# Rounds of two slots in an attention stage: which PSUM banks the units take by turns, and where scores and conversions stand

## The chip, the cores and the metric

One core of a Trainium2 chip runs the whole program. Its engines are TensorE (PE, with its weight loads shown apart as PEld), VectorE (DVE), ScalarE (ACT), GpSimd (POOL) and SyncE (SP), which issues the DMAs. The metric is the device time of one execution in microseconds (us); the time of a kernel is the median of its runs.

## The reference

Attention with heads mixed before and after the softmax, then two MLPs on the result (B=4, H=12, S=448, D=64; 1792 tokens of 768, hidden 2048; everything in float32):

```python
scores = scale * np.matmul(q, k.transpose(0, 1, 3, 2))
scores = np.einsum('bhij,hg->bgij', scores, w_pre)
scores = scores - np.max(scores, axis=-1, keepdims=True)
attn = np.exp(scores)
attn = attn / (np.sum(attn, axis=-1, keepdims=True) + 1e-09)
attn = np.einsum('bhij,hg->bgij', attn, w_post)
x = np.matmul(attn, v)                      # then (tokens, heads * D)
x = np.maximum(x @ w1_in, 0) ** 2 @ w1_out
h = x @ w2_in
out = (h * np.clip(h + 3, 0, 6) / 6) @ w2_out
```

## The kernel before, in words

**Stages.** The four batches are worked in two groups of two (`gi` 0 and 1). Each group has an attention stage (about 4 to 220 us and 690 to 890 us of the span) and then its MLPs (`Mlps` to 690, `Blocks` to the end, which saves products by sums of blocks). In the MLPs each matrix is split into a high and a low part, and three products stand for one in float32.

**Chunks, tiles, slots.** A group's queries come in eight chunks of 110 or 118 rows. A chunk is cut into tiles of 10 query rows times 12 heads (a last one of 8 rows), 90 tiles in all; a slot is two tiles, 45 slots. A tile goes through these steps:

- *Score* (`score`, line 186; products in line 183): for a chunk and two heads, eight matmuls into two PSUM banks; ACT copies one bank (line 189) and DVE the other (line 191) into the chunk's buffer `s`. Six scores make a chunk. There are two buffers `s`, so chunk 3 writes where chunk 1 was, and its copies must wait until SP's DMAs have fetched chunk 1's last tiles.
- *Fetch* (`fetch`, line 210): a DMA on SP reads a tile's rows of all heads out of `s` into `t`, five slots ahead.
- *Premix* (`premix`, line 222): eight matmuls for a slot with `w1f`, into two banks; then DVE's maximum (`top`, line 237), ACT's exponential with its sum (`soft`, line 246), DVE's reciprocal (`invert`, 254 and 255), POOL's weights scaled by it (`scale`, line 266).
- *Postmix* (`postmix`, line 278): eight matmuls for a tile, into one bank; `keep` copies it into `a`, for even tiles on ACT (line 293), for odd ones on DVE (line 295).
- *Values* (`values`, line 308): once a chunk's tiles are kept, 48 matmuls with V into each of two banks, which DVE copies into `xr` (line 318). The last chunk's come after the rounds, as `closing`.

**Banks.** PSUM has eight banks, held as four tags of two: "bm" and "by" take the premixes by turns, "bs" the scores, "bo" the postmixes, and, in rounds, the values too. A unit that takes a tag waits until the copies of what was there before have read it.

**Order.** Everything is written in the order in which each engine does it; nothing is rescheduled. From slot 1 (first group) or 3 (second group) on, `two_slots` (line 454) works two slots as one round: 22 rounds in the first group and 21 in the second. A round has two premixes, up to three scores, the values if a chunk is complete, and then a quad: the four postmixes of its two slots. Below, M is a premix of a slot, S a score, V a chunk's values, O one tile's postmix. A round with two scores is M S M S O O O O on PE; in one with three, the third comes after the O. `plan` (line 363) spreads a chunk's scores evenly over the slots from five before the end of the chunk two back to six before its own first tile, and puts the DMAs of q three slots ahead of their score. In a round, the first score of its first slot comes after the first premix, the next after the second, and any others at the round's end.

**Weights.** The first group's MLP weights come as 64-bit floats and are converted to 32 bits (`convert`, lines 658 to 667) and split into `wh` (ACT, line 693) and `wl` (DVE, line 694). For the first unit this is done in three steps during the attention stage (`early`, line 631), one in each round with values from slot 23 on: loads (chunk 3's values), first half (chunk 4's), second half, store and split (chunk 5's). In those rounds the step stands behind the values, and ahead of `soft(m + 3)`, the exponentials of the round's second premix.

**The entry into the MLP.** After `run` come the closing values, then the hidden products (`hidden`, line 730; matmuls in line 736): 18 matmuls for a block of 128 hidden units and one batch.

Of the kernel before, what the change touches and what calls it, by code (L numbers as in the profile page):

```python
# [70 lines left out]
def attention_mlp_kernel(ctx: ExitStack, tc, qT, kT, v, w_pre, w_post, mask, w1_in, w1_out, w2_in, w2_out, outT):  # L71
# [63 lines left out]
    class Attention:  # L135
        def __init__(self, gi):
            self.gi = gi
            self.batches = list(range(gi * NB, gi * NB + NB))
            self.chunks = [(b, ci) for b in self.batches for ci in range(len(CH))]
            self.tiles, self.first, self.tb = [], [], []  # L140
            for c, (b, ci) in enumerate(self.chunks):
                r0, n, nt, nl = CH[ci]
                self.first.append(len(self.tiles))
                self.tiles += [(c, t, RI if t < nt else nl) for t in range(nt + (nl > 0))]
            self.first.append(len(self.tiles))
            self.n = -(-len(self.tiles) // 2)
            self.live, self.ss, self.aa, self.ap, self.xr = {}, {}, {}, None, None
            self.ks, self.n_raw, self.raw, self.at, self.late = None, 0, None, {}, False
            if gi == 0:
                self.first_opening()  # L150
            self.plan()
# [34 lines left out]
        def score(self, c, k):  # L186
            out = [bank("bs" if self.ap else "bm", f"ps_s{self.gi}_{c}_{2 * k + e}") for e in range(2)]
            self.products(c, k, out)
            nc.scalar.activation(self.s(c)[:, 2 * k, :], out[0][:, :S], AF.Copy)  # L189
            if self.ap:  # L190
                nc.vector.tensor_copy(self.s(c)[:, 2 * k + 1, :], out[1][:, :S])
            else:
                nc.scalar.activation(self.s(c)[:, 2 * k + 1, :], out[1][:, :S], AF.Copy)
# [77 lines left out]
        def postmix(self, i):  # L271
            if i >= len(self.tiles):
                return
            c, t, ni = self.tiles[i]
            pt, w2s = self.live.pop(("w", i))
            o = bank("bo", f"ps_o{self.gi}_{i}")
            for q in range(JC):
                nc.tensor.matmul(  # L278
                    o[:JP, q * G * ni:(q + 1) * G * ni], lhsT=pt[:, q * JP:(q + 1) * JP],
                    rhs=w2s[:, :G * ni], start=True, stop=True)  # L280
            self.live["o", i] = o
# [81 lines left out]
        def plan(self):  # L363
# [11 lines left out]
            for c in range(1, nch):  # L375
# [5 lines left out]
                if c == 1:  # L381
                    when = [2 * k // nk for k in range(nk)]
                else:
                    low = last[c - 2] - FETCH + 1
                    when = [low + k * (top - low + 1) // nk for k in range(nk)]
                for j in range(2):
                    put(when[j * KP] - 3, self.fetch_q, c, j)
# [11 lines left out]
            for v in range(NV):  # L399
                put(1 + 3 * v, self.fetch_v, self.batches[0], v)  # L400

# [52 lines left out]
        def two_slots(self, m, early):  # L454
# [11 lines left out]
            visits = [[w for w in work if w[0].__name__ == "score"] for work in (first, second)]  # L466
            for (fn, (c, k)) in visits[0][1:]:
                assert self.first[c] // 2 - FETCH > m
            ready = [visits[0].pop(0)] if visits[0] else []
            rest = visits[0] + visits[1]  # L470

            def visit(work):
                if work:
                    fn, args = work.pop(0)
                    fn(*args)
# [11 lines left out]
            visit(ready)  # L487
# [12 lines left out]
            visit(rest)  # L500
            on(self.top_of, m + 3, 1)
            for fn, args in first + second:
                if fn.__name__ == "values":
                    fn(*args, "bo")
                    if early:
                        early.pop(0)()
                    on(self.soft, m + 3)
            self.postmix(2 * m)
# [3 lines left out]
            self.postmix(2 * m + 1)  # L512
            self.keep(2 * m + 1)
            on(self.scale, m + 2, 1)
            if ("m", m + 3) in self.live:
                self.soft(m + 3)
            self.postmix(2 * m + 2)
# [3 lines left out]
            self.postmix(2 * m + 3)  # L521
            self.keep(2 * m + 3)
            on(self.scale, m + 3, 1)
            while rest:
                visit(rest)
            do("fetch_v", first + second)

        def run(self, ap, behind, beside=None, early=None):
# [6 lines left out]
            for m in range(self.n + 1):  # L535
                two = m >= PAIRED[self.gi > 0] and (m - PAIRED[self.gi > 0]) % 2 == 0 and m + 1 < self.n
# [62 lines left out]
    class Mlps:  # L599
        def __init__(self, gi, att):  # L600
# [6 lines left out]
            self.arena, self.ready, self.late, self.scaled, self.unit0 = None, {}, [], set(), None  # L607
# [21 lines left out]
        def early(self):  # L629
# [16 lines left out]
            return [load, lambda: convert(0), lambda: (convert(1), self.store(0), self.split(0))]  # L646
# [83 lines left out]
        def hidden(self, which, fc, e, wh, wl, hp=None):  # L730
            cols = slice(e * S, (e + 1) * S)
            hp = hp or bank("bm", f"ps_h{self.gi}_{which}_{fc}_{e}")
            k = 0
            for c in range(KC):
                for lw, rw in ((wh, self.xh), (wl, self.xh), (wh, self.xl)):
                    nc.tensor.matmul(  # L736
                        hp[:, :S], lhsT=lw[:, c * P:(c + 1) * P], rhs=rw[:, c, cols],
                        start=(k == 0), stop=(k == 3 * KC - 1))
                    k += 1
            return hp  # L740

# [53 lines left out]
        def run(self, mp, behind):  # L795

            rest = None
            for n, (kind, which, m, _) in enumerate(self.units):
# [19 lines left out]
                if kind == "h":  # L818
# [14 lines left out]
                    hp = self.hidden(which, m, 0, wh, wl)  # L833
# [32 lines left out]
    class Blocks(Mlps):  # L866
# [117 lines left out]
        def early(self):  # L984
            return []

# [261 lines left out]
    with tc.manual_schedule():  # L1248
# [5 lines left out]
        for gi in range(groups):  # L1254
            last = gi > 0 and gi == groups - 1
            mlp = (Blocks if last else Mlps)(gi, att)
            with tc.tile_pool(name=f"ap{gi}", bufs=1, reuse_waits="tile") as ap:
                rest = att.run(ap, mlp.opening(), mlp.beside if last else None, mlp.early())

                for m, step in enumerate(att.closing()):  # L1260
# [90 lines left out]
```

## Time and profile before

| | |
|---|---|
| median of three runs | 1301.23 us (1299.87 to 1302.35) |
| the profiled execution, its own time | 1300.42 us |
| its span | 1298.6 us |
| granted clock of PE, mean | 0.999 |
| busy: PE, PE's loads | 1278.5 us (98%), 1097.8 us (85%) |
| busy: DVE, ACT, POOL | 918.9 (71%), 653.5 (50%), 270.5 us (21%) |
| chain that ended last, by engine | PE 95%, DMA 2%, ACT 1%, DVE 1% |
| the same chain, attention's lines | O 12%, S 6%, V 6%, M 5% |

The span is what the hardware profiler recorded between the first and the last instruction of one execution; the execution's own time is 1.8 us longer. Busy time of an engine is that in which at least one of its records is open. PE's matmuls overlap, so a matmul that waits a little for its bank leaves no gap in the busy time; a row of a timeline joins equal instructions that follow each other, and "x32" says how many. The time from the start of one such row to the start of the next shows what the busy time doesn't. In brackets stands the idle time of the engine before a row, and what ended it.

### The profile page before, as it was taken

What the parts mean: (1) busy time and instruction counts of PE and PEld (TensorE: products, weight loads), DVE (VectorE), ACT (ScalarE), POOL (GpSimd) and SP (SyncE); (2) the same over time, 40 slices, a digit from 0 to 9 for tenths busy, and PEclk for the clock granted to TensorE, in tenths of its full rate; (3) what the DMA queues carried; (4) which work ended last, traced back from release to release, by engine and by line L of the source; (5) the groups of instructions that cost most, each with busy time, mean ns of one, the idle gap of its engine ahead of it and who ended that gap; (6) DMA issues with size and microseconds to landing.
All of it is one profiled execution on the core that took longest, in us unless ns stands there. A gap on an engine that the chain in (4) does not pass through costs nothing.

```text
span 1298.6 us, 23568 instructions
## 1 busy us (share of the span) xinstructions
PE 1278.5 (98%) x8788; PEld 1097.8 (85%) x8788; DVE 918.9 (71%) x1554; ACT 653.5 (50%) x1260; POOL 270.5 (21%) x349
## 2 busy tenths in 40 slices
PE   8999989999999999999999999999999999999998
PEld 4677668999999999998895677778999999999998
DVE  5666666777766587875555666664977897799975
ACT  5555555555322355542425554555768555446652
POOL 2111113343200033310101334352001120001422
PEclk9999999999999999999999999999999999999999
DMA  6644422767786676677774776666877856785442
GB/s 201 185 135 149 131 105 99 206 202 208 240 279 186 191 227 202 206 233 234 257 250 152 230 230 219 195 213 231 275 246 222 272 184 203 232 286 175 126 132 95
DMA packets 131090, 261.10 MB, mean 201 GB/s; under 512 B 13728, under 2 KB 99872, under 8 KB 130976
## 3 DMA queue, kind: packets, MB, share of 16 engines
q1 hardware_dynamic: 127520, 254.09, 61.3%
q10 hardware_dynamic: 3456, 5.51, 1.2%
q8 instruction: 69, 1.13, 0.4%
q14 instruction: 45, 0.37, 0.1%
HBM read 151.02 MB, written 69.99 MB: 170 GB/s over the span
## 4 chain that ended last, share of the span: by engine, by line
PE 95%; DMA 2%; ACT 1%; DVE 1%; issue 0%; SPq 0%; ACTq 0%; POOL 0%; DVEq 0%
PE ps_h L736 18%; PE ps_a L750 18%; PE ps_w L1046 16%; PE ps_y L1146 16%; PE ps_o L278 12%; PE ps_s L183 6%; PE ps_v L308 6%; PE ps_m L222 5%; DMA t<-s 1%; DMA q<-in_dram 1%; ACT p L246 0%; DMA first<-in_dram 0%; DVE mx L237 0%; ACT a L293 0%; ACT s L189 0%
## 5 line engine op out<-in xcount | busy, mean ns | idle before, releaser
L278 PEld LDWEIGHTS ps_o<-w2s,p 128*112 128x112 f32 x1440 | 157.4, 178 | 40.2 <-issue 30.0
L278 PE MATMUL ps_o<-w2s,p 128*112 128x120 f32 (+1 forms) x1440 | 172.9, 274 | 7.8 <-ACT a L293 6.8
L750 PE MATMUL ps_a<-gh,wh 128*128 128x448 f32 x384 | 140.2, 365 | 0.0
L750 PE MATMUL ps_a<-gh,wl 128*128 128x448 f32 x384 | 138.7, 361 | 0.0
L694 DVE TENSOR_TENSOR wl<-arena,wh 128x768 fp32r<-128x768 f32 x63 | 61.8, 981 | 105.4 <-ACT wh L693 102.1
L266 POOL TENSOR_SCALAR w2s<-w2f,rz 128x120 f32<-128x120 f32 x180 | 65.3, 370 | 333.0 <-DVE rz L255 212.0
L1135 POOL TENSOR_TENSOR o<-gi,o 128x448 fp32r<-128x448 f32 x28 | 57.4, 2052 | 336.8 <-ACT o L1130 230.0
L246 ACT ACTIVATE p<-ps_m,mx 128x448 f32<-128x448 f32 x180 | 112.6, 632 | 24.9 <-DVE mx L237 21.8
L237 DVE TENSOR_REDUCE mx<-ps_m 128x1 f32<-128x448 f32 x180 | 105.2, 616 | 16.8 <-PE ps_m L222 16.1
L693 ACT ACTIVATE wh<-arena 128x768 fp32r<-128x768 f32 x63 | 52.8, 839 | 121.1 <-PE ps_a L750 113.7
L1146 PE MATMUL ps_y<-o,wx 128*128 128x448 f32 x504 | 105.4, 362 | 0.0
L1146 PEld LDWEIGHTS ps_y<-o,wx 128*128 128x128 f32 x504 | 94.5, 187 | 6.3
L189 ACT ACTIVATE s<-ps_s 128x448 f32<-128x448 f32 x87 | 47.1, 541 | 103.2 <-PE ps_s L183 98.1
L1146 PE MATMUL ps_y<-o,wh 128*128 128x448 f32 x336 | 98.7, 362 | 0.0
L728 POOL TENSOR_TENSOR gl<-g,gh 128x448 fp32r<-128x448 f32 x40 | 53.6, 1341 | 205.3 <-ACT gh L727 159.7
L295 DVE COPY a<-ps_o 112x480 f32<-112x480 f32 (+1 forms) x90 | 58.9, 654 | 47.5 <-PE ps_o L278 47.2
L293 ACT ACTIVATE a<-ps_o 112x480 f32<-112x480 f32 (+1 forms) x90 | 51.7, 575 | 75.6 <-PE ps_o L278 75.5
L222 PE MATMUL ps_m<-t,w1f 64*64 64x448 f32 x720 | 87.5, 546 | 1.8 <-POOL w2s L266 1.3
L183 PE MATMUL ps_s<-k,q 64*64 64x448 f32 x672 | 86.3, 555 | 2.6 <-ACT s L189 2.6
L750 PE MATMUL ps_a<-gl,wh 128*128 128x448 f32 x240 | 86.7, 361 | 0.0
L308 PEld LDWEIGHTS ps_v<-a,v 112*64 112x64 f32 x1536 | 73.8, 137 | 11.6 <-issue 9.2
L750 PEld LDWEIGHTS ps_a<-gh,wh 128*128 128x128 f32 x384 | 72.1, 188 | 10.0 <-issue 5.6
(117 smaller groups left out, 2892.0 us busy)
## 6 DMA issues: line engine op xcount, KB each, us to landing
arena<-in_dram SPq DMA_DIRECT2D x63, 768.0 KB
t<-s SPq DMA_DIRECT2D x176, 210.0 KB
keep<-arena SPq DMA_DIRECT2D x63, 384.0 KB
pr<-keep SPq DMA_DIRECT2D x88, 192.0 KB
wr<-sums_in SPq DMA_DIRECT2D x64, 192.0 KB
wr<-sums_out SPq DMA_DIRECT2D x64, 192.0 KB
low<-wl SPq DMA_DIRECT2D x28, 384.0 KB
wr<-keep SPq DMA_DIRECT2D x48, 192.0 KB
```

What stands on the lines that cost most here:

```text
L183: nc.tensor.matmul(out[e][to:to + half_p, :S], lhsT=q[own, to:to + half_p], rhs=keys[own], start=True, stop=True)
L222: nc.tensor.matmul(out[a][to:to + half_p, :S], lhsT=w1f[own], rhs=t[own], start=True, stop=True)
L237: nc.vector.reduce_max(mx[:, a:a + 1], out[a][:, :S], axis=AX.X, negate=True)
L246: nc.scalar.activation(pt, o[:, :S], AF.Exp, bias=mx[:, a:a + 1], accum_out=z[:, a:a + 1])
L266: nc.gpsimd.tensor_scalar(w2s[:, :G * ni].rearrange("p (g i) -> p g i", g=G), w2f[:, a, :, :ni], rz[:, a:a + 1], 1.0, op0=ALU.mult, op1=AL ...
L278: nc.tensor.matmul(o[:JP, q * G * ni:(q + 1) * G * ni], lhsT=pt[:, q * JP:(q + 1) * JP], rhs=w2s[:, :G * ni], start=True, stop=True)
L308: nc.tensor.matmul(xo[e * D:(e + 1) * D, k * n:(k + 1) * n], lhsT=self.v[:, q, g, :], rhs=self.aa[c][:, q, g, :n], start=(q == 0), stop=(q ...
L694: nc.vector.tensor_tensor(out=wl, in0=self.wr(n), in1=f(wh), op=ALU.subtract)
L736: nc.tensor.matmul(hp[:, :S], lhsT=lw[:, c * P:(c + 1) * P], rhs=rw[:, c, cols], start=(k == 0), stop=(k == 3 * KC - 1))
L750: nc.tensor.matmul(acc[d, e][:, :S], lhsT=lw[:, wc], rhs=rw[fc, e], start=(fc == 0 and k == 0), stop=(fc == NF - 1 and k == 2))
L1046: nc.tensor.matmul(to[:, :S], lhsT=lw[:, wc], rhs=rw, start=(d == 0 and j == 0), stop=(d == DB - 1 and j == 2))
L1146: nc.tensor.matmul(self.acc[d][:, :S], lhsT=lw[:, wc], rhs=rw, start=(u == 0 and q == 0 and j == 0), stop=(u == NU // 2 - 1 and q == UF - ...
```

## The change

In rounds, scores, values and both pairs of a quad's postmixes take "bs" and "bo" by turns, by one counter (`in_turn`); before, scores always had "bs", and values and postmixes "bo". The two products of a pair share a tag, as before.

The places of a chunk's scores come from a list (`places`): each slot's possible places in a round, after the first premix (V), after the second (W) or at the end (C), and the last six before the chunk's first fetch are used; the first of them that lies in the slot of the earlier chunk's last fetches is left out. The q DMAs are issued four slots ahead, not three.

In rounds with values, the order is now: exponentials of the second premix, conversion step, values (before: values, conversion step, exponentials). The early conversion has four steps, as `split(0)` is one of its own, so they fall to the values of chunks 3, 4, 5 and 6.

`begin` puts the first nine of the first block's 18 hidden matmuls ahead of the closing values, in the first group alone.

```diff
+        def in_turn(self):
+            self.turn = 1 - self.turn
+            return ("bs", "bo")[self.turn]
+
-        def score(self, c, k):
-            out = [bank("bs" if self.ap else "bm", f"ps_s{self.gi}_{c}_{2 * k + e}") for e in range(2)]
+        def score(self, c, k, tag=None):
+            out = [bank(tag or ("bs" if self.ap else "bm"), f"ps_s{self.gi}_{c}_{2 * k + e}") for e in range(2)]
...
-        def postmix(self, i):
+        def postmix(self, i, tag="bo"):
...
-            o = bank("bo", f"ps_o{self.gi}_{i}")
+            o = bank(tag, f"ps_o{self.gi}_{i}")
...
-                    low = last[c - 2] - FETCH + 1
-                    when = [low + k * (top - low + 1) // nk for k in range(nk)]
+                    places = self.places(last[c - 2] - FETCH + 1, top)[-nk:]
+                    when = [slot for slot, _ in places]
+                    self.place.update({(c, k): place for k, (_, place) in enumerate(places)})
                 for j in range(2):
-                    put(when[j * KP] - 3, self.fetch_q, c, j)
+                    put(when[j * KP] - 4, self.fetch_q, c, j)
...
+        def rounds(self, m):
+            m -= PAIRED[self.gi > 0]
+            return None if m < 0 else m % 2
+
+        def places(self, low, top):
+
+            out = []
+            for m in range(low, top + 1):
+                at = self.rounds(m)
+                if at is None:
+                    out += [(m, "A")] * (2 if m == low + 1 else m > low)
+                    continue
+                if at == 0 or m > low:
+                    out.append((m, "VW"[at]))
+                if at == 1:
+                    out.append((m, "C"))
+            return out
...
-            visits = [[w for w in work if w[0].__name__ == "score"] for work in (first, second)]
-            for (fn, (c, k)) in visits[0][1:]:
-                assert self.first[c] // 2 - FETCH > m
-            ready = [visits[0].pop(0)] if visits[0] else []
-            rest = visits[0] + visits[1]
-
-            def visit(work):
-                if work:
-                    fn, args = work.pop(0)
-                    fn(*args)
+            visits = [w for w in first + second if w[0].__name__ == "score"]
+
+            def visit(place):
+                for fn, args in visits:
+                    if self.place[args] == place:
+                        fn(*args, self.in_turn())
...
             on(self.premix, m + 2)
             on(self.top, m + 2, False)
-            visit(ready)
+            visit("V")
...
-            visit(rest)
+            visit("W")
             on(self.top_of, m + 3, 1)
             for fn, args in first + second:
                 if fn.__name__ == "values":
-                    fn(*args, "bo")
+                    on(self.soft, m + 3)
                     if early:
                         early.pop(0)()
-                    on(self.soft, m + 3)
-            self.postmix(2 * m)
+                    fn(*args, self.in_turn())
+            tag = self.in_turn()
+            self.postmix(2 * m, tag)
...
-            self.postmix(2 * m + 1)
+            self.postmix(2 * m + 1, tag)
...
+            tag = self.in_turn()
             if ("m", m + 3) in self.live:
                 self.soft(m + 3)
-            self.postmix(2 * m + 2)
+            self.postmix(2 * m + 2, tag)
...
-            self.postmix(2 * m + 3)
+            self.postmix(2 * m + 3, tag)
...
-            while rest:
-                visit(rest)
+            visit("C")
...
-            return [load, lambda: convert(0), lambda: (convert(1), self.store(0), self.split(0))]
+            return [load, lambda: convert(0), lambda: (convert(1), self.store(0)), lambda: self.split(0)]
...
-        def hidden(self, which, fc, e, wh, wl, hp=None):
+        def hidden(self, which, fc, e, wh, wl, first=0, end=KC):
...
+        def begin(self):
+            if 0 in self.ready:
+                self.head.append(self.hidden(0, 0, 0, *self.ready[0], end=KC // 2))
...
                 rest = att.run(ap, mlp.opening(), mlp.beside if last else None, mlp.early())
 
+                mlp.begin()
                 for m, step in enumerate(att.closing()):
                     step()
```

The order of instructions shows this at three places. First PE in the first group, the round that does tiles 10 to 13 (`ps_m` premix, `ps_s` score, `ps_o` postmix); before:

```order
L222 MATMUL ps_m_16_520<-t_6_200,w1f 64x448 x2
L222 MATMUL ps_m_17_521<-t_7_203,w1f 64x448 x2
L183 MATMUL ps_s_3_0_533<-k_80,q_3_0_410 64x448
L183 MATMUL ps_s_3_1_534<-k_80,q_3_0_410 64x448
L183 MATMUL ps_s_3_0_533<-k_80,q_3_0_410 64x448
L183 MATMUL ps_s_3_1_534<-k_80,q_3_0_410 64x448
L278 MATMUL ps_o_10_543<-w2s_5_0_462,p_5_0_438 112x120 x4
L278 MATMUL ps_o_11_554<-w2s_5_1_470,p_5_1_440 112x120 x4
L278 MATMUL ps_o_12_568<-w2s_6_0_486,p_6_0_473 112x120 x4
L278 MATMUL ps_o_13_579<-w2s_6_1_494,p_6_1_475 112x120 x4
L183 MATMUL ps_s_3_2_587<-k_80,q_3_0_410 64x448
```

The same place after the change:

```order
L226 MATMUL ps_m_16_520<-t_6_200,w1f 64x448 x2
L226 MATMUL ps_m_17_521<-t_7_203,w1f 64x448 x2
L282 MATMUL ps_o_10_534<-w2s_5_0_454,p_5_0_430 112x120 x4
L282 MATMUL ps_o_11_545<-w2s_5_1_462,p_5_1_432 112x120 x4
L282 MATMUL ps_o_12_559<-w2s_6_0_478,p_6_0_465 112x120 x4
L282 MATMUL ps_o_13_570<-w2s_6_1_486,p_6_1_467 112x120 x4
L226 MATMUL ps_m_18_580<-t_8_226,w1f 64x448 x2
L226 MATMUL ps_m_19_581<-t_9_229,w1f 64x448 x2
L183 MATMUL ps_s_3_0_588<-k_80,q_3_0_402 64x448
L183 MATMUL ps_s_3_1_589<-k_80,q_3_0_402 64x448
```

Chunk 3's first score left this round, in which chunk 1's last tiles are fetched, and stands in the next, behind its first premix.

Second ACT in the first group, the round with chunk 5's values (`p` exponentials, `unit` the scaled weights, `wh` the split, `a` copies of postmixes); before:

```order
L246 ACTIVATE p_37_0_2120,z_37_2119<-ps_m_74_2102,mx_37_2108 128x448
L246 ACTIVATE p_37_1_2122,z_37_2119<-ps_m_75_2103,mx_37_2108 128x448
L658 ACTIVATE unit_1878<-raw_1_1558 128x384
L693 ACTIVATE wh_0_2186<-unit_1878 128x768
L246 ACTIVATE p_38_0_2191,z_38_2190<-ps_m_76_2113,mx_38_2124 128x448
L246 ACTIVATE p_38_1_2193,z_38_2190<-ps_m_77_2114,mx_38_2124 128x448
L293 ACTIVATE a_6_2072<-ps_o_70_2195 112x48x10
L293 ACTIVATE a_6_2072<-ps_o_72_2214 112x48x10
```

And after the change:

```order
L250 ACTIVATE p_37_0_2120,z_37_2119<-ps_m_74_2102,mx_37_2108 128x448
L250 ACTIVATE p_37_1_2122,z_37_2119<-ps_m_75_2103,mx_37_2108 128x448
L250 ACTIVATE p_38_0_2128,z_38_2127<-ps_m_76_2113,mx_38_2124 128x448
L250 ACTIVATE p_38_1_2130,z_38_2127<-ps_m_77_2114,mx_38_2124 128x448
L678 ACTIVATE unit_1823<-raw_1_1503 128x384
L297 ACTIVATE a_6_2072<-ps_o_70_2191 112x48x10
L297 ACTIVATE a_6_2072<-ps_o_72_2210 112x48x10
```

The second slot's exponentials moved ahead of the conversion, and the making of `wh` left this round for the one of chunk 6's values.

Third PE at the end of the first group's attention, after the change (`ps_v` the closing values, `ps_h` the hidden product):

```order
L282 MATMUL ps_o_89_2525<-w2s_44_1_2500,p_44_1_2481 112x96 x4
L755 MATMUL ps_h_0_0_0_2536<-xh_2229,wh_0_2337 128x448
L755 MATMUL ps_h_0_0_0_2536<-xh_2229,wl_0_2338 128x448
L755 MATMUL ps_h_0_0_0_2536<-xl_2230,wh_0_2337 128x448
...
L312 MATMUL ps_v_7_0_2546<-a_7_2398,v_173 64x118 x24
L312 MATMUL ps_v_7_1_2578<-a_7_2398,v_173 64x118 x24
```

Nine hidden matmuls, of which three are shown, stand between the last postmix and the closing values; before, all 18 came behind the values.

## Rows read from the trace of the kernel before

**Rows 1.** The page, PE's busy tenths in 40 equal slices of the span.

```profile
PE   8999989999999999999999999999999999999998
```

**Rows 2.** Busy by engine (us, instructions), one round and one stretch; then clock, DMA share, GB/s.

```profile
114.08:121.21 7.13, 7.13 (x66) 4.61 (x65) 5.36 (x12) 4.57 (x12) 1.42 (x5) 1.00 0.14 53
...
175.00:200.00 25.00, 21.57 (x280) 17.52 (x274) 14.75 (x33) 12.47 (x33) 6.35 (x12) 0.93 0.40 149
```

**Rows 3.** PE's timeline, 105.5 to 118 us: start, duration, operation, count, [wait before].

```profile
105.97 0.98 PE L183 MATMUL ps_s<-k,q 64*64 64x448 f32 x8
...
110.37 3.78 PE L278 MATMUL ps_o<-w2s,p 128*112 128x120 f32 x32
114.08 0.98 PE L222 MATMUL ps_m<-t,w1f 64*64 64x448 f32 x8
114.89 0.93 PE L183 MATMUL ps_s<-k,q 64*64 64x448 f32 x8
115.64 0.93 PE L222 MATMUL ps_m<-t,w1f 64*64 64x448 f32 x8
...
117.50 0.77 PE L278 MATMUL ps_o<-w2s,p 128*112 128x120 f32 x5
```

**Rows 4.** PE's timeline, 69 to 72 us, premix, score and values without waits.

```profile
70.70 0.93 PE L183 MATMUL ps_s<-k,q 64*64 64x448 f32 x8
71.56 0.69 PE L308 MATMUL ps_v<-a,v 112*64 112x110 f32 x10
```

**Rows 5.** PE's timeline, three narrow windows inside the quad that starts at 110.37.

```profile
111.39 0.47 PE L278 MATMUL ps_o<-w2s,p 128*112 128x120 f32 x3
...
112.00 0.53 PE L278 MATMUL ps_o<-w2s,p 128*112 128x120 f32 x2
...
112.21 0.43 PE L278 MATMUL ps_o<-w2s,p 128*112 128x120 f32 x2
```

**Rows 6.** Postmix matmuls and their loads by line: ns least/median/most, first and last start.

```profile
L278 PEld LDWEIGHTS ps_o<-w2s,p x1440: 172/177/311, 22.6 to 884.7; 128*112 128x112 f32 x180
L278 PE MATMUL ps_o<-w2s,p x1440: 262/266/447, 22.6 to 884.8; 128*112 128x120 f32 x176, 128*112 128x96 f32 x4
```

**Rows 7.** ACT's timeline, 111 to 119 us: copy of a first product, exponential, last score's copy.

```profile
111.48 0.58 ACT L293 ACTIVATE a<-ps_o 112x480 f32<-112x480 f32 x1 [0.35 <-PE ps_o L278]
...
117.10 0.63 ACT L246 ACTIVATE p<-ps_m,mx 128x448 f32<-128x448 f32 x1
...
117.73 0.53 ACT L189 ACTIVATE s<-ps_s 128x448 f32<-128x448 f32 x1
```

**Rows 8.** PE's and ACT's timelines beside the values of chunks 4 and 5.

```profile
159.30 1.04 PE L278 MATMUL ps_o<-w2s,p 128*112 128x120 f32 x8 [0.76 <-ACT a L293]
...
183.38 0.84 ACT L693 ACTIVATE wh<-unit 128x768 fp32r<-128x768 f32 x1 [5.31 <-DVE unit L667]
...
186.06 3.45 PE L278 MATMUL ps_o<-w2s,p 128*112 128x120 f32 x16 [3.29 <-ACT a L293]
```

**Rows 9.** PE's timeline at the scores that wait for fetches, both groups.

```profile
27.78 1.13 PE L183 MATMUL ps_s<-k,q 64*64 64x448 f32 x8 [0.91 <-ACT s L189]
...
44.08 1.90 PE L278 MATMUL ps_o<-w2s,p 128*112 128x120 f32 x16
47.15 2.16 PE L278 MATMUL ps_o<-w2s,p 128*112 128x120 f32 x16 [1.18 <-ACT a L293]
...
702.93 1.10 PE L183 MATMUL ps_s<-k,q 64*64 64x448 f32 x8 [0.65 <-ACT s L189]
...
722.73 2.15 PE L278 MATMUL ps_o<-w2s,p 128*112 128x120 f32 x16 [0.92 <-ACT a L293]
```

**Rows 10.** PE's timeline at the end of the first group's attention.

```profile
215.02 5.06 PE L308 MATMUL ps_v<-a,v 112*64 112x118 f32 x96 [0.74 <-DVE a L295]
...
220.32 0.37 PE L736 MATMUL ps_h<-xh,wl 128*128 128x448 f32 x1
220.52 0.37 PE L736 MATMUL ps_h<-xl,wh 128*128 128x448 f32 x1
```

More of the change, by code (lines that the diff above doesn't have):

```diff
@@ L147, in __init__ @@
             self.live, self.ss, self.aa, self.ap, self.xr = {}, {}, {}, None, None
-            self.ks, self.n_raw, self.raw, self.at, self.late = None, 0, None, {}, False
+            self.ks, self.n_raw, self.raw, self.at, self.late, self.turn, self.place = None, 0, None, {}, False, 1, {}
             if gi == 0:
@@ L535, in run @@
             for m in range(self.n + 1):
-                two = m >= PAIRED[self.gi > 0] and (m - PAIRED[self.gi > 0]) % 2 == 0 and m + 1 < self.n
+                two = self.rounds(m) == 0 and m + 1 < self.n
                 if two:
@@ L606, in __init__ @@
             self.W = w1_in.shape[-1]
-            self.arena, self.ready, self.late, self.scaled, self.unit0 = None, {}, [], set(), None
+            self.arena, self.ready, self.late, self.scaled, self.unit0, self.head = None, {}, [], set(), None, []
         def raw(self, n):
@@ L728, in split_g @@
             nc.gpsimd.tensor_tensor(out=gl, in0=g, in1=f(gh), op=ALU.subtract)
-        def hidden(self, which, fc, e, wh, wl, hp=None):
+        def hidden(self, which, fc, e, wh, wl, first=0, end=KC):
             cols = slice(e * S, (e + 1) * S)
[L732 to L735, printed above, removed]
+            hp = self.head.pop(0) if first else bank("bm", f"ps_h{self.gi}_{which}_{fc}_{e}")
+            for c in range(first, end):
+                for k, (lw, rw) in enumerate(((wh, self.xh), (wl, self.xh), (wh, self.xl))):
                     nc.tensor.matmul(
                         hp[:, :S], lhsT=lw[:, c * P:(c + 1) * P], rhs=rw[:, c, cols],
-                        start=(k == 0), stop=(k == 3 * KC - 1))
-                    k += 1
-            return hp
+                        start=(c == 0 and k == 0), stop=(c == KC - 1 and k == 2))
+            return hp
+        def begin(self):
+            if 0 in self.ready:
+                self.head.append(self.hidden(0, 0, 0, *self.ready[0], end=KC // 2))
         def project(self, u, e, wh, wl, acc):
@@ L832, in run @@
                                         [P, S], F32R, tag=tag, name=f"g{part}{nm}_{fc}_{e}", bufs=bufs)
-                    hp = self.hidden(which, m, 0, wh, wl)
+                    hp = self.hidden(which, m, 0, wh, wl, first=KC // 2 if self.head else 0)
                     done = self.act(which, m, 0, hp)
@@ L985, in early, with begin @@
             return []
+        def begin(self):
+            pass
         def split_x(self, c, e):
```

## The prediction

> **What bounds the kernel now.** TensorE (PE) does. I read four views, in this order. The page's busy shares in 40 slices show where PE is not full: the two attention stages, slices 1 to 7 and 22 to 28 [rows 1]; in the MLPs it is full, and of those the change touches only the entry into the first. The table by stretches then shows that a full PE is no proof of a dense one: a round of attention from one quad of postmixes to the next takes 7.13 us and PE is busy for all of it, though its matmuls wait inside (matmul records overlap, so short waits vanish in them) [rows 2]. DVE with 5.36 and ACT with 4.57 us of that round are not the bound. So I measured from start to start of the units in PE's timeline [rows 3], against stretches where nothing waits [rows 4]. Last, narrow windows inside one quad and the rows of single waits.
>
> **A: the postmixes' wait for their bank.** A quad is four products of eight matmuls, 32 in all. Before, all four take the pair "bo", so the third needs the copy of the first to be done. From the start of the first matmul to that of the last a quad takes 3.78 less the 0.266 of one matmul, 3.51 us [rows 3, 6]. Without a wait it would be: the first half of a quad, 16 matmuls, has 1.90 at 44.08, less 0.27, so 1.63 [rows 9]; 16 further steps of (0.47 - 0.266) / 2 = 0.102 us [rows 5, 6] make 1.64; together 3.27. The difference is 0.24 us a quad. Where it sits: the third product starts 0.21 after the last matmul of the second (0.10 would do), just when ACT's copy, which ran from 111.48, has freed the bank [rows 5, 7]; its next step takes 0.43 - 0.27 = 0.16 [rows 5]; and the fourth has the rest. After the change the second pair of products takes the pair that the last score or the values had, whose copies were issued a quad earlier. The program has 22 rounds of two slots in the first group and 21 in the second: 43 x 0.244 = **10.5 us**. All quads that I read have the 3.71 us from start to next unit, but for the few of C and D.
>
> The nearest rule that speaks against it: the row shows steps of 0.10 us, though the load before each matmul takes 0.177 us, so loads do run beside matmuls here [rows 5, 6]. The Trainium skill, "TensorE: Matmul & The Clock Gate", section "Packing small matmuls — row/col tiling", says that a weight load overlaps with matmuls in flight only when their row groups differ, and a postmix weight covers all 128 rows. By that rule the slow steps would be the loads', and would stay; by the row they are the wait's.
>
> **B: the scores' wait for their bank.** A unit of premix or score without a wait has 0.81 us when first after a quad, 0.75 in the middle, and 0.86 before a quad or values [rows 3, 4]. Premix, score, premix, score would be 0.81 + 0.75 + 0.75 + 0.86 = 3.17; it takes 117.50 - 114.08 = 3.42: 0.25 too many. Score, premix, score, premix, score would be 3.92 and takes 4.40: 0.48 too many [rows 3]. Each score waits for the copies of the score before, as "bs" is the only pair. By the program the first kind stands in 14 rounds, the second in 11: 14 x 0.25 + 11 x 0.48 = **8.8 us**. With turns a score finds the pair of two units before. In the round with three scores, the one after the quad meets the pair of the quad's first two products, long copied.
>
> **C: conversions.** In the round with chunk 5's values the second half of the quad starts at 186.06 after a wait of 3.29 and takes 3.45, where a first half takes 1.90: 4.8 us [rows 8, 9]. ACT's copies stand behind the two exponentials, and these behind the making of wh, which started at 183.38 [rows 8], after DVE's conversion. Part of the 3.45 is the clock: PE was granted 0.93 on average over 175 to 200 us [rows 2], below full only after that idle time; with no idle time it stays up. The round with chunk 4's values has a wait of 0.76 for the same reason [rows 8], about 0.8 with the slower restart. The change puts the exponentials ahead of the conversion and makes wh a step of its own in the round of chunk 6's values. What is then late? The values' copies on DVE come behind the conversion (its four DVE steps are some 2 us), but values run for 5 us and the first half of the quad for 1.7 before anything asks for their pair, so I cost that at nothing; if the cover were gone it would be 1 to 2 us in each of three rounds. Term: **5.6 us**, bounds 2 and 6.
>
> **D: scores that wait for fetches.** A score's copy writes a buffer whose fetches from two chunks earlier must have landed, and the quad behind it waits. The rows: 0.91 at 27.78; 1.18 at 47.15 with 0.26 more in the second half; 0.92 at 722.73 with 0.25 more; and 0.65 at 702.93 with one like it at the next score [rows 9]. That makes 1.0 + 1.4 + 1.2 + 1.3 to 1.7. The change puts the first score of a chunk a round later (order, first place) and, in the second group's opening, between postmixes. Two scores fewer fit before the deadline there, so the last ones land nearer to the fetch that they feed; the nearest slack I see is about a round. q's fetch is issued one slot earlier on SP, moved past two issues of t; t is fetched more than a round ahead, so nothing waits for it. Term **5.1 us**, bounds 2 and 5.5.
>
> **E: the entry into the first MLP.** The closing values wait 0.74 us for DVE's last copy, about 0.8 with the restart [rows 10]. Nine hidden matmuls of 0.20 us each [rows 10] now stand before them: 1.8 us of work that has to be done anyway, longer than the wait. They need only the first batch's half of x, split long before, and the first unit of weights, split in the round of chunk 6's values. Term **0.8 us**, bounds 0 and 0.9.
>
> Elsewhere nothing changes: each engine has as many instructions as before, and POOL's order is the same.
>
> **The sum.** 10.5 + 8.8 + 5.6 + 5.1 + 0.8 = 30.8 us. The profiled execution took 1300.42 us, so 1269.6; the median of the runs is 0.8 above it: **1270 us**. In the rounds I find no more than about 4 us of further waits, so the least is about 1266, and 1264 with the scatter of single runs.
>
> **What could be late in the place of the waits.** A round of 7.13 us becomes one of 7.13 - 0.24 - 0.25 = 6.64; DVE's 5.36 is then 81% of it, ACT's 4.57 is 69%. The new nearest wait: the quad's third product needs ACT's copy of the round's last score. That copy ended at 117.73 + 0.53 = 118.26 [rows 7]. In the shorter round the quad would start at 117.25 and ask for the bank half a quad later, at 118.99. So 0.7 us of slack, 0.5 if ACT does not get quicker by the 0.25.
>
> **Rivals.**
> 1. *The loads hold the pace.* If the slow steps inside a quad belong to the loads, as the rule above has it, only the late start of the third and the fourth product goes, some 0.12 of the 0.24 a quad: 43 x 0.12 = 5.2 us are not won, 1275. For: the step of 0.16 has no copy beside it. Against: the same product has it at 0.10 a few steps on, at equal loads [rows 5, 6], and a half quad of 1.90 runs without it [rows 9]. Chance 0.09.
> 2. *The copies come late.* The slack of 0.5 to 0.7 us is used up because ACT's copy stands behind exponentials which wait for DVE's maxima. Rounds would wait 0.3 us on average: 43 x 0.3 = 13, 1283. For: ACT does the score's copy right behind an exponential [rows 7]. Against: both engines have a fifth of the round idle. Chance 0.12.
> 3. *Only the banks count.* C, D and E give nothing, as the same waits come back a round later (the conversion's DVE steps before the values' copies; the later scores against their fetch): 19.3 remain, 1281. Against: the waits there are for work that now stands elsewhere. Chance 0.06.
> 4. *Slower.* The third product waits in every round until the two exponentials behind the last premix are through, because ACT serves them ahead of the copy. The one before the copy took from 117.10 to 117.73 with its read [rows 7]; two take 1.3 us, and with the wait for their maxima that rival 2 has (0.3) 1.6; less the slack of 0.5, 1.1 a round: 43 x 1.1 = 47 against the 30.8, about 1317. It decides from 33.4 / 43 = 0.78 us a round on. Against: by the program's order that copy stands ahead of those exponentials. Chance 0.02.
> That the alternation does nothing because some unit falls back on the pair just used would leave D and C alone, 1290; but by the code every unit of a round but the premixes draws its pair from the one counter: 0.01.
>
> **How the numbers follow.** The forecast has 0.70. Range: it holds the forecast with all bounds (1266 to 1276), rival 1, rival 3 and rival 2: **1264 to 1285**. A measurement of this kernel tells 0.2% (2.6 us) from no change. Faster 0.95; same 0.03 (all terms at their lower ends and late copies on top); slower 0.02.
>
> **What would show it.** Right: quads at 3.5 us from start to next unit; four units at 3.2; five at 3.9; rounds of about 6.6; no wait of PE over 0.5 us at chunk 4's and 5's values nor where chunk 3's first score was; granted clock 1.00 there; hidden matmuls before the closing values. Wrong: waits of PE for ACT's score copy or DVE's xr copy inside quads (rival 2), 0.16 steps without any wait (rival 1), a wait of over 1 us at the values of chunks 3 to 6 (rival 3), rounds above 7.1 (rival 4).

## The result, and the profile after

The changed kernel takes 1270.13 us (1269.17 to 1273.39), the one before 1301.79 us beside it: a ratio of 0.9756 (95% interval 0.9723 to 0.9788), 31.7 us less. The forecast was 1270. That the total came out does not make the terms right, and two were not.

The page of the changed kernel, its busy times, PE's share in 40 slices and the granted clock:

```profile
PE 1259.6 (99%) x8788; PEld 1089.8 (86%) x8788; DVE 918.5 (72%) x1554; ACT 651.0 (51%) x1260; POOL 269.7 (21%) x349
...
PE   8999999999999999999999999999999999999998
...
PEclk9999999999999999999999999999999999999999
```

The sixth slice, the only one inside the attention stages that had an 8 [rows 1], shows a 9 now. A round in PE's timeline, the counterpart of [rows 3], and that round in the table by stretches, the counterpart of [rows 2]:

```profile
97.50 0.98 PE L226 MATMUL ps_m<-t,w1f 64*64 64x448 f32 x8
98.31 0.93 PE L183 MATMUL ps_s<-k,q 64*64 64x448 f32 x8
99.06 0.93 PE L226 MATMUL ps_m<-t,w1f 64*64 64x448 f32 x8
99.81 0.94 PE L183 MATMUL ps_s<-k,q 64*64 64x448 f32 x8
100.68 3.53 PE L282 MATMUL ps_o<-w2s,p 128*112 128x120 f32 x32
104.14 0.98 PE L183 MATMUL ps_s<-k,q 64*64 64x448 f32 x8
...
108.07 3.50 PE L282 MATMUL ps_o<-w2s,p 128*112 128x120 f32 x32
```

```profile
97.50:104.14 6.64, 6.64 (x65) 4.49 (x64) 5.26 (x12) 4.59 (x12) 1.10 (x4) 1.00 0.55 192
```

Four units take 100.68 - 97.50 = 3.18 us (3.42 before), the quad 3.46 to the next unit (3.71), five units 108.07 - 104.14 = 3.93 (4.40). The round is 6.64 us where it was 7.13; DVE with 5.26 us is 79% of it.

The round with chunk 5's values, the counterpart of [rows 8], and the entry into the first MLP, of [rows 10]:

```profile
161.74 1.74 PE L226 MATMUL ps_m<-t,w1f 64*64 64x448 f32 x16
163.40 4.74 PE L312 MATMUL ps_v<-a,v 112*64 112x110 f32 x96
168.07 3.54 PE L282 MATMUL ps_o<-w2s,p 128*112 128x120 f32 x32
171.53 1.74 PE L226 MATMUL ps_m<-t,w1f 64*64 64x448 f32 x16
```

```profile
196.37 0.37 PE L755 MATMUL ps_h<-xl,wh 128*128 128x448 f32 x1
196.67 5.06 PE L312 MATMUL ps_v<-a,v 112*64 112x118 f32 x96
201.66 0.47 PE L755 MATMUL ps_h<-xh,wh 128*128 128x448 f32 x1
```

No wait is left in either. What is left in the attention stages stands in the second group's, above all in its opening; the waits of PE from 668 to 870 us (total, times, longest), and its timeline there, to hold against [rows 9]:

```profile
PE ps_m L226 <- DMA t<-s: 1.7, 2, 1.6
PE ps_s L183 <- ACT s L193: 1.4, 1, 1.4
PE ps_v L312 <- DVE a L299: 0.7, 1, 0.7
...
```

```profile
674.12 0.98 PE L183 MATMUL ps_s<-k,q 64*64 64x448 f32 x8 [1.38 <-ACT s L193]
...
697.82 0.97 PE L226 MATMUL ps_m<-t,w1f 64*64 64x448 f32 x4 [0.17 <-DMA t<-s]
...
705.49 1.35 PE L226 MATMUL ps_m<-t,w1f 64*64 64x448 f32 x6 [1.56 <-DMA t<-s]
```

The profiled execution took 1273.39 us, 3.3 above the median, so its span is only 27.0 shorter. By starts of PE's rows, the first group's attention gained 201.2 - 182.8 = 18.4 us, from its first postmix to the 19th hidden matmul, so that the first block's 18 count on both sides; the second group's gained 199.5 - 192.9 = 6.6, from its first postmix to the first product of the blocks; the opening 1.7, the MLPs 0.3. (The 1.7 are not the change's: the kernel before with one part of the change put in, and the opening untouched, also reached its first postmix at 20.7 us.) By the sum the first group should have gained 18.6, the second 12.2 (21 x 0.244 of A, half of B, 2.7 of D). So the first question was whether those premixes' waits belong to the change or to one execution.

### The profile page after: what moved, and what is told of

Read it like the earlier page. It is cut to its first block, busy times and chain, and to the rows that moved or that the text cites. A ratio compares the mean times of both kernels' runs of the same rounds, so it can differ in the third digit from the quotient of the medians.

```text
span 1271.6 us, 23639 instructions
## 1 busy us (share of the span) xinstructions
PE 1259.6 (99%) x8788; PEld 1089.8 (86%) x8788; DVE 918.5 (72%) x1554; ACT 651.0 (51%) x1260; POOL 269.7 (21%) x349
## 4 chain that ended last, share of the span: by engine, by line
PE 97%; DMA 2%; ACT 0%; DVE 0%; issue 0%; SPq 0%; ACTq 0%
PE ps_h L755 18%; PE ps_a L772 18%; PE ps_w L1071 16%; PE ps_y L1171 16%; PE ps_o L282 12%; PE ps_v L312 6%; PE ps_s L183 6%; PE ps_m L226 6%; DMA t<-s 1%; DMA first<-in_dram 0%; DMA outT_dram<-ot 0%; ACT ot L790 0%; ACT p L250 0%; SPq L163 0%; DVE y L1180 0%
## 5 line engine op out<-in xcount | busy, mean ns | idle before, releaser
L282 PEld LDWEIGHTS ps_o<-w2s,p 128*112 128x112 f32 x1440 | 150.7, 177 | 26.2 <-issue 17.9
L282 PE MATMUL ps_o<-w2s,p 128*112 128x120 f32 (+1 forms) x1440 | 159.9, 269 | 0.0
```

The costliest lines, as they stand in the source:

```text
L282: nc.tensor.matmul(o[:JP, q * G * ni:(q + 1) * G * ni], lhsT=pt[:, q * JP:(q + 1) * JP], rhs=w2s[:, :G * ni], start=True, stop=True)
```

## The experiments

### Once more, and the side loads of the second group

The changed kernel again, and a version in which the loads of weights whose sums POOL makes beside the second group's attention start at slot 8, not 2, and stand closer together ("..." stands for lines of code not shown here):

```diff
-            j, o = (i - 1) // 4, (i - 1) % 4
...
+            for j in range(len(todo)):
+                at = i - FIRST_PR - (38 - FIRST_PR) * j // (len(todo) - 1)
...
```

> The changed kernel once more, for a second profile of it. In the first profile the second group's attention gained 6.6 us where the sum has 12.2, with waits of premixes for fetches (1.56 and 0.3 us and some shorter ones), a wait of 1.38 us for a score's copy behind ACT's wait for an output store, and late entries into values. Theory chance: these waits belong to one execution; in this profile they are gone or elsewhere, the second stage gains 11 us or more and the whole stands near 1268 in the profile too. Theory fetch chain: the shorter rounds of the opening ask for tiles that SP has not issued or the DMAs have not landed; then the premixes of the rounds at slots 5 and 7 of the second group wait again, by 1 to 3 us in sum, and the stage gains 6 to 9. Median about 1270 in either case.

> The changed kernel with the second group's side work moved: the loads of weights whose sums are made beside the attention (pr, 0.75 MB a slot in four) start at slot 8 and not at slot 2, somewhat closer together, so that in the opening of the second group SP's queue and the DMAs have the tiles alone. Theory fetch chain: the premixes' waits for tiles at slots 5 and 7 shrink or vanish; 1 to 4 us faster than the change, about 1267. Theory chance: no difference, 1270. Against it: POOL has the same work in fewer slots, and could delay the scaled weights of postmixes: some us slower.

Again: 1269.97 us (0.9757, 0.9735 to 0.9779: here and below, the ratio to the kernel before beside it, and its 95% interval). Its profiled execution took 1273.4 and had a wait for tiles again (0.9 us); the four others took 1268.77 to 1270.03. With the side loads later: 1271.39 us (0.9765, 0.9743 to 0.9787), and the profiled execution, 1271.69, had no such wait over 0.5 us there. From the start of the 7th postmix of the second group to that of the 15th it took 17.9 us, against 22.0 and 21.1 in the two profiles of the changed kernel. That speaks for the traffic in that opening as the cause. It is not shown, as a third run of the changed kernel, below, had 18.7 us there and no such wait in its profile. By their times (1268.3 to 1270.95 us), the eleven executions of the changed kernel without a profile seldom pay for these waits, and the later loads won nothing.

### The turns undone, whole and in part

Scores always on "bs", values and postmixes on "bo"; and, apart from it, only the turn inside a quad taken away:

```diff
-                        fn(*args, self.in_turn())
+                        fn(*args, "bs")
...
-                    fn(*args, self.in_turn())
-            tag = self.in_turn()
+                    fn(*args, "bo")
+            tag = "bo"
             self.postmix(2 * m, tag)
...
-            tag = self.in_turn()
```

The second kernel has the last of these edits alone.

> The turns undone: scores always on bs, values and postmixes always on bo; placement, conversions and the early hidden matmuls stay. Theory banks (A and B of the sum): quads are back at 3.71 us to the next unit, four units at 3.4 and five at 4.4, and the time rises by 19 us to about 1289. Rival, the waits were for the copies' engines and not for the bank: the quads stay at 3.47, and the time at 1270 to 1275.

> Only the turn inside a quad undone: both pairs of a quad's postmixes take the same tag, which still changes from quad to quad; scores and values keep their turns. Theory A: every quad gets its 0.244 us back and the scores' units stay dense: 43 x 0.244 = 10.5 us, about 1280.5. Rival, the loads hold the pace: the quad's slow steps were only half the bank's, the cost is 5 us, about 1275. If the fetches of the second group were hidden by longer quads, it costs less there: 8 to 9 us in all.

With one tag a quad: 1280.71 us (0.9839, 0.9817 to 0.9862), 10.7 above the changed kernel on the same chip. Its timeline shows the quad back at 108.02 - 104.31 = 3.71 us and the five units still at 111.94 - 108.02 = 3.92:

```profile
104.31 3.78 PE L282 MATMUL ps_o<-w2s,p 128*112 128x120 f32 x32
108.02 0.98 PE L183 MATMUL ps_s<-k,q 64*64 64x448 f32 x8
...
111.94 0.36 PE L282 MATMUL ps_o<-w2s,p 128*112 128x120 f32 x1
```

It is so in every quad: of the 39 that are not followed by another quad, all take 3.43 to 3.47 us to the next unit in the changed kernel, and 37 take 3.71 to 3.73 here (the other two 3.82 and 4.01). That settles A: the whole 0.25 us a quad is the bank's. The loads beside the matmuls don't hold the pace.

With no turns: 1291.53 us (0.9922, 0.9901 to 0.9943), 21.6 above the changed kernel. The four units are back at 3.41 (103.37 to 106.78). The 10.8 above the other kernel are 2 more than B's 8.8, and the first group's waits name most of it:

```profile
103.37 0.98 PE L226 MATMUL ps_m<-t,w1f 64*64 64x448 f32 x8
...
106.78 3.78 PE L282 MATMUL ps_o<-w2s,p 128*112 128x120 f32 x32
```

```profile
PE ps_o L282 <- DVE xr L322: 1.6, 3, 0.9
```

Three quads wait for the copies of the values, which now come behind the conversion's steps on DVE. The prediction had looked for this wait in the change and costed it at nothing; with turns that is right.

### One other part undone at a time

The conversions as before (values, step, exponentials; the split joined to the third step); the placement as before; the early hidden matmuls taken away:

```diff
-                    on(self.soft, m + 3)
+                    fn(*args, self.in_turn())
                     if early:
                         early.pop(0)()
-                    fn(*args, self.in_turn())
+                    on(self.soft, m + 3)
...
```

```diff
-                    places = self.places(last[c - 2] - FETCH + 1, top)[-nk:]
-                    when = [slot for slot, _ in places]
+                    low = last[c - 2] - FETCH + 1
+                    when = [low + k * (top - low + 1) // nk for k in range(nk)]
...
```

```diff
-                mlp.begin()
```

> Only the conversions undone: values, then the conversion step, then the second slot's exponentials, and the split joined to the third step; turns, placement and the early hidden matmuls stay. Theory, the terms add up: the waits of 3.3 and 0.8 us inside the quads after the values of chunks 4 and 5 are back, and the time is 5.6 us longer, about 1275.6. Rival, the turns alone would have hidden most of it: the quad's second pair now takes the values' banks, which the copies free before the conversion starts, so the late copies of the first pair hold up only the unit after the quad; then 0 to 2.5 us, 1270 to 1272.5.

> Only the placement of scores undone: spread evenly as before, q fetched three slots ahead; turns, conversions and the early hidden matmuls stay. Theory, the terms add up: waits of about 1 to 1.4 us where chunk 3's first score stands in the round of chunk 1's last fetches, in both groups, and about 1.5 in the second group's slots 1 and 2; 5.1 us longer, about 1275. Rival, the turns hide part: 2 to 3 us. Rival, the new placement is what made the second group's premixes wait for tiles, and gave back what it won: no change, 1270.

> Only the early start of the first hidden product undone: all 18 matmuls stand behind the closing values. Theory: the closing values wait about 0.75 us for DVE's last copy again, 0.8 us longer, about 1270.8. Rival, the hidden matmuls only moved a wait (they wait for their own operands or bank): no change.

Conversions: 1272.92 us (0.9778, 0.9758 to 0.9798), not clear of the changed kernel. PE's timeline and ACT's beside chunk 5's values:

```profile
163.58 4.74 PE L312 MATMUL ps_v<-a,v 112*64 112x110 f32 x96
168.25 3.53 PE L282 MATMUL ps_o<-w2s,p 128*112 128x120 f32 x32
171.71 2.14 PE L226 MATMUL ps_m<-t,w1f 64*64 64x448 f32 x16
```

```profile
170.75 0.84 ACT L713 ACTIVATE wh<-unit 128x768 fp32r<-128x768 f32 x1 [5.31 <-DVE unit L687]
...
172.72 1.03 ACT L297 ACTIVATE a<-ps_o 112x480 f32<-112x480 f32 x2
```

ACT makes wh late and copies the postmixes only at 172.72, 9.14 us after the start of the values. Before the change it was 9.14 us as well:

```profile
176.20 4.74 PE L308 MATMUL ps_v<-a,v 112*64 112x110 f32 x96
...
185.34 0.57 ACT L293 ACTIVATE a<-ps_o 112x480 f32<-112x480 f32 x1
```

Yet the quad runs through in 3.46: its second pair has the values' banks and asks for none of these copies. Only the premixes after it are 0.4 us longer. From the start of the first group's 63rd postmix to that of the 87th, which holds the values of chunks 5 and 6, it took 40.59 us, the changed kernel 39.87; from the 15th to the 63rd, with those of chunks 3 and 4, the two agree. So C is worth 0.7 us once the turns are there.

Placement: 1276.66 us (0.981, 0.9785 to 0.9835), 6.9 above the changed kernel (0.981 against 0.9757). Chunk 3's first score in the first group, PE and ACT:

```profile
40.46 1.90 PE L282 MATMUL ps_o<-w2s,p 128*112 128x120 f32 x16
47.06 3.51 PE L282 MATMUL ps_o<-w2s,p 128*112 128x120 f32 x16 [4.71 <-ACT s L193]
```

```profile
46.37 0.54 ACT L193 ACTIVATE s<-ps_s 128x448 f32<-128x448 f32 x1 [5.34 <-DMA t<-s]
```

Before the change, with [rows 9] for the quad:

```profile
45.99 0.54 ACT L189 ACTIVATE s<-ps_s 128x448 f32<-128x448 f32 x1 [1.59 <-PE ps_o L278]
```

The score's copy runs at 46.37, about when it did before the change (45.99). The quad starts 3.6 us sooner, at 40.46 and not 44.08 [rows 9] (1.7 of it the opening's), and so waits 4.71 us, not 1.18. The half quad behind it takes 3.51 against 1.90: after that idle time PE was granted 0.50 of its clock, the lower of its two levels, from 47.0 to 50.5 us. The old placement would have given back here what the turns had won until then. All of it is the first group's: from its first postmix to the 19th hidden matmul it took 189.7 us, in the three profiles of the changed kernel 182.8 to 183.9. The second group took 190.4 to the first product of the blocks, the changed kernel 188.8 to 192.9, with the waits for tiles in the longer ones, so what the placement won there is not shown.

Entry: 1273.0 us (0.9774, 0.9752 to 0.9797), not clear in the time. In its trace the wait is there:

```profile
196.87 5.06 PE L312 MATMUL ps_v<-a,v 112*64 112x118 f32 x96 [0.74 <-ACT arena L678]
```

From the start of the last quad to the 19th hidden matmul, so with the same work on both sides, it took 12.84 us, the changed kernel 12.07: E is 0.77 us.

### One part alone

The kernel before with the turns alone, and with the conversions alone (the edits above, the other way round):

> The kernel before with the turns alone: scores, values and both pairs of postmixes alternate between bs and bo; placement, order of conversions and the entry into the MLP are as before. Theory, the terms add up as in the prediction: A and B, 19.3 us, are won, about 1281.5. Theory of overlap, from the runs with one part undone: the turns also hide the conversions (undoing those alone cost 1 to 3 us and not 5.6), while the score that waits for a fetch gives back more in shorter rounds (its wait grew from 1.2 to 4.7 us); so 5.6 more from C and some 2 less from D: about 1278, with no wait over 1 us at the values of chunks 4 and 5 and one of over 4 us at chunk 3's first score.

> The kernel before with the new order of conversions alone: exponentials, conversion step, values, and the split as a fourth step; banks, placement and entry as before. Theory of the prediction: 5.6 us faster, about 1295.5, and the waits of 3.3 and 0.8 us are gone. Theory of overlap: without turns the quad shares its banks with the values, whose copies now come behind the conversion's steps on DVE, so a wait of 0.5 to 1 us for these copies stands in each of three rounds in its place: 4 us faster, about 1297.

Turns alone: 1282.27 us (0.9848, 0.9833 to 0.9863), 20 us faster than before. The number is that of the plain sum, the trace that of the overlap. The waits of PE in the first group, and in the second:

```profile
PE ps_o L282 <- ACT s L193: 4.0, 2, 3.5
```

```profile
PE ps_o L282 <- ACT s L193: 3.8, 1, 3.8
PE ps_s L183 <- ACT s L193: 2.7, 3, 1.4
```

The waits at the conversions are gone, with the old order of conversions; those at the scores that wait for fetches have grown to 3.5 and 3.8 us. The 1278 of the theory of overlap had counted only the first of these two.

Conversions alone: 1299.21 us (0.9973, 0.9959 to 0.9987), 3.5 faster. Where the wait of 3.29 was, one for the values' copies stands:

```profile
183.36 3.75 PE L282 MATMUL ps_o<-w2s,p 128*112 128x120 f32 x32 [0.89 <-DVE xr L322]
```

In this profile chunk 3's first score held up its quad for 2.54 us, as its copy ran at 46.80. In the four profiles with the old placement that copy ran at 45.3 to 46.8 us, while the quad that it held up started between 40.5 and 44.1: the later the quad, the shorter the wait, but for the spread of the landing.

### Two tries at more

In the second group, chunk 6's values behind the last postmix, as cover for the closing values' wait of 0.7 us; and, beside a third run of the changed kernel, only the first three side loads moved (to slots 6, 9 and 12):

```diff
-                put(last[c] + 2, self.values, c, range(NV))
+                if self.gi == 0 or c < nch - 2:
+                    put(last[c] + 2, self.values, c, range(NV))
...
```

```diff
...
+                at = i - (FIRST_PR[j] if j < 3 else 2 + 4 * j)
...
```

> The changed kernel with one thing more: in the second group the values of the chunk before the last stand behind the last postmix, ahead of the closing values, as cover for the wait of 0.7 us for DVE's last copy, which the change leaves there. Theory: the wait of the closing values vanishes, 0.8 us faster, about 1269.2. Rival: the later copies of chunk 6's values delay the sums that the blocks start with, and as much is lost behind the values: no change or up to 2 us slower.

> The changed kernel a third time, beside the next one on the same chip. Its runs fell between 1268.8 and 1275.2 us together with those of its near variants, and the profiled ones near 1273.4; 1270 to 1272 in the median.

> The changed kernel with only the first three of the side loads of the second group moved (from slots 2, 6 and 10 to slots 6, 9 and 12); the others keep their slots, so that POOL's work is not denser later. Theory fetch chain: in the profile the premixes' waits for tiles in the second group's opening vanish, 3 us; the runs' spread shrinks, and the median falls by 1 to 3 us below that of the changed kernel beside it. Rival: as with all side loads moved, the runs without a profile do not have those waits, and the median stays within 1 us.

Chunk 6's values late: 1271.95 us (0.9769, 0.9747 to 0.9791), no gain. The closing values no longer wait, but the last quad does, for POOL's scaled weights, which the values had covered:

```profile
851.88 3.48 PE L282 MATMUL ps_o<-w2s,p 128*112 128x120 f32 x32 [0.87 <-POOL w2s L270]
```

The changed kernel a third time: 1270.39 us (0.9745, 0.9723 to 0.9766). With three loads moved: 1268.79 us (0.974, 0.9719 to 0.9762), 1.6 lower, and no wait for tiles in its profile. The second group's attention took 187.0 us there, 12.5 less than before the change, where the sum had 12.2; in the three profiles of the changed kernel it gained 6.6, 7.4 and 10.7. The two intervals lie over each other, so that this beats the changed kernel is not shown; both beat the one before.

## Why the prediction was right, and where it was not

**The bound and A.** PE was the bound, and a full PE hid short waits. One reading on the way was wrong: the page's row has only slices 1, 6 and 40 below a 9 [rows 1], not slices 1 to 7 and 22 to 28; where PE waits came out of the other three views. A was 10.5 us by the sum and 10.7 by the run that undoes it. Rival 1 (the loads) is out: by it half of the 0.25 would have stayed, and all of it went with the bank. The Trainium skill ("TensorE: Matmul & The Clock Gate", "Packing small matmuls — row/col tiling") has it that a weight load overlaps with matmuls in flight only where their row groups differ. This trace does not agree: loads of 0.177 us over all 128 rows go with steps of 0.10 us [rows 5, 6]. Rival 2 is out too: no wait for ACT's or DVE's copies is left inside a quad, and the round came out at 6.64 us as worked out. Rival 3 had the waits come back at C, D and E; they did not, though one score of the second group's opening now waits 1.0 us longer than before, for a reason that no term had (last section). Rival 4 needed rounds over 7.1.

**B.** 8.8 by the sum; undoing it after A cost 10.8. Of the 2 too many, 1.6 are the values' copies behind the conversion, which are no part of B in the kernel before.

**C failed as a term.** The step "ACT's copies stand behind the two exponentials" was right; the step from there to 5.6 us of its own was not. The quad waited for these copies only because its second pair took the banks of the first, which is the very thing that A removes. With turns the order of conversions is worth 0.7 us in the trace; without them 3.5 us.

**D was mis-sized in the other direction.** I priced it by the waits before: 2.4 us in the first group and 2.7 in the second. Undone it cost 6.9, by the traces all of it in the first group; the second group's part is not shown. A wait whose end is set by a fetch does not keep its length when the work ahead of it gets shorter. The two errors have one root, that the terms were added as if independent. In the first group C's 4.9 too many and D's 3.4 to 4.5 too few nearly cancel, and that is luck: undone, the five terms cost 10.7, 10.8, 0.7, 6.9 and 0.8, 29.9 us in all against the 30.8 of the sum.

**E** was 0.8 by the sum and is 0.77 in the trace; the time alone cannot tell it.

**The second group.** "Nothing waits for it", said of the tiles, held for most rounds but not for the second group's first ones, where in some executions the tiles come late. In the profile of the result that is likely what cost the 3.3 us above the median.

## What to carry to other kernels

Several waits that end in the same resource are one term: take the resource away in thought first, then price what remains. A wait that ends at an event which the change does not move, as the landing of a fetch here, grows by what is won ahead of it; such waits are priced last, against the shortened schedule. One run with a part undone and one with it alone show such overlaps; either by itself would have looked like a clean price.

## What was not expected

The wait of 1.38 us at 674.12, where the same score waited 0.37 before the change, stands behind ACT's issue of two output stores. In the first profile of the changed kernel that pair took 1.84 us; before the change, and with one tag a quad, 0.82:

```profile
670.41 1.84 ACTq L792 DMA_DIRECT2D outT_dram<-ot  x2
672.30 0.63 ACT L250 ACTIVATE p<-ps_m,mx 128x448 f32<-128x448 f32 x1 [1.92 <-DMA outT_dram<-ot]
```

The order of these instructions is the same in all three kernels, and DVE had made the data by 670.70. The other traces narrow it down. The second store of the pair took 0.39 us in the four profiles of kernels without the turn inside a quad, and 0.96 to 1.99 us in the ten with it. In these ten, and in none of the four, a 16 KB packet of the kind that the profile calls "instruction", by its name a piece of the program on its way to the core, is in flight when this store is issued, and the store ends 0.2 to 0.4 us after the packet has landed. The DMA queues from 670.4 to 672.3 us (packets, MB, share of the 16 DMA engines):

```profile
q10 hardware_dynamic: 255, 0.40, 57.2%
q8 instruction: 1, 0.02, 4.4%
```

So the program's own fetch probably holds the store up, and the turn inside a quad probably moved that fetch to this place; no run moves it by itself. The other surprise is the spread: executions of the changed kernel lie between 1268.3 and 1273.4 us. The two profiled ones with waits for tiles in the second group's opening took 1273.4, the one without 1270.5; that this makes the whole spread is likely, not shown.
